# Twenty-eight more fill matmuls in front of batch 0, and another gate for batch 2's q loads

## The chip, the cores and the metric

The kernel runs on one core of a Trainium2 chip. The metric is the device time of one execution in microseconds, as the median of several runs. The engines are named as the profile names them: PE is TensorE (PEld its weight loads), DVE is VectorE, ACT is ScalarE, POOL is GpSimd, and SP is SyncE, which here only issues transfers.

## The reference

Linear attention over 8 batches, 8 heads, 576 positions and 64 columns a head, followed by a normalised two-layer block with a residual:

```
q_s = softmax(q, over head_dim);  k_s = softmax(k, over seq)
kv  = einsum('bhsd,bhse->bhde', k_s, v)
x   = einsum('bhsd,bhde->bhse', q_s, kv)      -> [8, 576, 512]
xn  = (x - mean) / sqrt(var + 1e-6) * g_ln
out = x + relu(xn @ w_ch1) @ w_ch2            w_ch1 [512, 2048], w_ch2 [2048, 512]
```

All inputs and the output are float32 in HBM; the kernel multiplies in bf16.

## The kernel before

**Tiling.** Each batch's first 512 positions form one unit of work ("c", 0 to 7), with position p*4+t on partition p; the remaining 64 positions of all batches form a ninth unit, which runs last. Of a unit, TensorE forms `pkv` (exp of k times v, line 252), VectorE scales it into `kv_sb` (line 260), TensorE forms `po` (exp of q transposed, times `kv_sb`, line 283), VectorE and ScalarE make the normalised `xn`, its transpose is `xnT`, and then come the products with w1 (`ph`, lines 406 and 421, each followed by a relu into `hT`) and with w2 (`pc`, line 466, for unit 0; seven-product form, line 513, for the others).

**Order.** All engines run in the order in which the program is written (a manual schedule). `first_batch()` writes the start by hand. After it, `run()` walks through the steps of one unit's two layers on TensorE, and lets side work of the next units in at given positions: a pair `(96, f)` calls f when the steps so far weigh 96. During unit 0's layers the side work contains unit 1's attention: casts of v at 94 (`cast_v`, line 153, into `vm`; `prep_kvrem`, lines 158 and 159, into `ekr` and `vr`), all of `pkv` at 96 (`kv_all`), `po` from 96.5. At 119 and 127 ScalarE takes the exp of unit 2's q (line 176), and between them, at 126, stands the transpose of unit 1's `xn` whose copy to `xnT` ScalarE makes (line 793).

**The start.** `first_batch()` issues q and k of batch 0 on SP and v, w1 and the rest of q on GpSimd, with small copies into `gate` that make GpSimd wait for q and for k before it issues more. TensorE gets fills: `warm(n)` writes n matmuls of 256 columns of a zero tile `junk` into a bank that nothing reads. There are four groups before unit 0's layers: 32 at the very start; 4 behind each of the two groups of transposes of exp(q) (`eq_pT`, line 791); 10 between `po` and the transposes of `xn` (line 901). Between the second and the third come `gps` (g_ln broadcast to all partitions, line 882), `z` (sums of exp(k), line 229), `pkv`, `po`. Unit 0's layers start with w1's first block of columns for position groups t=0 and t=1, then blocks two to four for t=0,1, and then all blocks for t=2,3.

**The loads after it.** GpSimd's queue takes, in this order: w1's blocks, w2's first two blocks (of four, four row groups each), batch 1's q, k, v and remainders (`load_second`), w2's third and fourth block (`load_w2(2)`, `load_w2(3)`), and then `load_third()`: a one-element copy on GpSimd into batch 2's q tile, and batch 2's v. Batch 2's q and k and their remainders (ktr, vtr) are issued on SP; the q load overwrites what the copy wrote, so it waits for the copy, and what stands behind it on SP waits with it. Batch 2's k and v share their buffers with batch 1's.

Of the kernel before, what the change touches and what calls it, by code (L numbers as in the profile page):

```python
# [20 lines left out]
def kernel(  # L21
# [16 lines left out]
    nc = tc.nc  # L38
# [41 lines left out]
    w2_sb = const.tile([P, KO2, DM], BF16)  # L80
# [9 lines left out]
    def load_w1(nb):  # L90
        cols = slice(nb * 512, nb * 512 + 512)
        nc.gpsimd.dma_start(w1_sb[:, :, cols], w1_src[:, :, cols])

    def load_w2(g4):
        rows = slice(4 * g4, 4 * g4 + 4)
        nc.gpsimd.dma_start(w2_sb[:, rows, :], w2_src[:, rows, :])
# [4 lines left out]
    raws = {}  # L101
# [62 lines left out]
    def new_eq(c):  # L164
        eqs[c] = (
            att.tile([P, T, H, D], BF16, tag="eq", name="eq"),
            sml.tile([P, T, H], FP32, tag="zq", name="zq"),
            sml.tile([P, T, H], FP32, tag="rq", name="rq"),
        )
        eqTs[c] = att.tile([P, T, NP, P], BF16, tag="eqT", name="eqT")  # L170
# [10 lines left out]
    def exp_qt(b, t):  # L181
        if t == 0 and b:
            new_eq(b)
        nc.scalar.activation(eqs[b][0][:, t], raws[b][2][:, :, t], AF.Exp)
# [27 lines left out]
    def exp_k0(j):  # L212
        hs = slice(2 * j, 2 * j + 2)
        if j == 0:
            eks[0] = raw.tile([P, T0, H, D], BF16, tag="vt", name="ek0", bufs=1)
        nc.scalar.activation(
            eks[0][0:P0, :, hs, :].rearrange("p t h d -> p h t d"), raws[0][0][0:P0, hs], AF.Exp
        )

    def k0_mm(j, t):  # L220
        hs = slice(2 * j, 2 * j + 2)
        return eks[0][0:P0, t, hs, :], raws["v0"][0:P0, hs, t, :], P
# [11 lines left out]
    def recip_z(src):  # L234
        rzk = sml.tile([P, 2], FP32, tag="rzk", name="rzk")
        nc.vector.reciprocal(rzk, src)
        return rzk

    def kv_mm(b, j, t):
        par = b % 2  # L240
        last = T if b else T0 - 1
        if j % 2 == 0 and t == 0:
            kvbox["p"] = att_ps.tile([P, 2, 256], FP32, tag="a", name="pkv")
        pkv = kvbox["p"]
        w = P + 1
        if b == 0:
            lhsT, rhs, w = k0_mm(j, t)
        elif t < T:
            lhsT, rhs = eks[b][:, t, 2 * j : 2 * j + 2, :], vm[:, par, t, j, 0 : P + 1]
        else:  # L250
            lhsT, rhs = ekr[:, par, 2 * j : 2 * j + 2, :], vr[:, par, j, 0 : P + 1]
        nc.tensor.matmul(  # L252
            pkv[:, j % 2, 0:w], lhsT, rhs, start=(t == 0), stop=(t == last)
        )
        if j % 2 == 1 and t == last:
            js = slice(j - 1, j + 1)
            rzk = recip_z(pkv[:, :, P]) if b else kvbox["rz", j // 2]
            for half in range(2):
                ps = slice(64 * half, 64 * half + 64)
                nc.vector.tensor_mul(  # L260
                    kv_sb[ps, b, js, ps], pkv[ps, :, ps],
                    rzk[ps].to_broadcast([64, 2, D]),
                )

    def start_x(c):
        xs[c] = (
            mlp.tile([P, T, DM], BF16, tag="x", name="x"),
            mlp.tile([P, T, 6], FP32, tag="st", name="st"),
            mlp.tile([P, T, DM], BF16, tag="xn", name="xn"),
            mlp.tile([P, T, 2], FP32, tag="mv", name="mv"),  # L270
        )
        xnTs[c] = mlp.tile([P, T, KO1, P], BF16, tag="xnT", name="xnT")
# [74 lines left out]
    def mean_x(c, t):  # L347
        nc.scalar.activation(
            scrap, pobox[c, t], AF.Copy, scale=-1.0 / DM, accum_out=xs[c][3][:, t, 0:1]
        )  # L350
# [330 lines left out]
    def warm(n, width=256):  # L681

        w = mm_ps.tile([P, 512], FP32, tag="m", name="warm")
        for _ in range(n):
            nc.tensor.matmul(w[:, 0:width], junk[:, 0:P], junk[:, 0:width], start=True, stop=True)  # L685
# [97 lines left out]
    def norm_q(b, t):  # L783
        eq, zq, rq = eqs[b]
        sum_q(b, t)
        nc.vector.tensor_mul(eq[:, t], eq[:, t], rq[:, t].to_broadcast([P, H, D]))  # L786
# [19 lines left out]
    def eq_pT(c, t, eng):  # L806
        pe_T(eqTs[c], eqs[c][0][:, t].rearrange("p h d -> p (h d)"), t, eng)
# [4 lines left out]
    def first_batch():  # L812

        nc.scalar.preload_act_table_set("natural_log_exp_and_others")
        raws[0] = (
            mlp.tile([P, H, T0, D], FP32, tag="hT", name="kt0", bufs=1), None,
            raw.tile([P, H, T, D], FP32, tag="qt", name="qt"),
        )
        k0, _, q0 = raws[0]
        v0 = mlp.tile([P, H, T0, D], BF16, tag="hs", name="v0", bufs=1)  # L820
        raws["v0"] = v0
        g_row = outp.tile([1, DM], FP32, tag="ot", name="g_row")

        def load_q0(half, eng=nc.sync):
            ts = slice(2 * half, 2 * half + 2)
            eng.dma_start(
                q0[:, :, ts],
                q[0, :, 0:SM, :].rearrange("h (p t) d -> p h t d", t=T)[:, :, ts],
            )

        def src0(x, h0, hn):
            return x[0, h0 : h0 + hn].rearrange("h (p t) d -> p h (t d)", t=T0)

        load_q0(0)
        for h0 in range(0, H, 2):
            nc.sync.dma_start(
                k0[0:P0, h0 : h0 + 2].rearrange("p h t d -> p h (t d)"), src0(k, h0, 2)
            )
            if h0 == 0:
                nc.sync.dma_start(  # L840
                    g_row, bass.AP(moe_g_ln.tensor, moe_g_ln.offset, [[0, 1], [1, DM]])
                )
        nc.vector.memset(junk, 0.0)
        nc.vector.memset(eps_ln, 1e-6)
        nc.vector.memset(ones, 1.0)
        nc.vector.memset(ones_f, 1.0)
        nc.vector.memset(bones, 0.0)
        nc.vector.memset(bones[0:64, 0:1], 1.0)
        nc.vector.memset(bones[64:P, 1:2], 1.0)
        nc.vector.memset(kv_sb, 0.0)  # L850
        make_identity(nc, ident)
        nc.gpsimd.tensor_copy(out=gate, in_=q0[:, 1, 0, 0:4])
        for h0 in (0, 4):
            nc.gpsimd.dma_start(
                v0[0:P0, h0 : h0 + 4].rearrange("p h t d -> p h (t d)"), src0(v, h0, 4)
            )
        nc.gpsimd.tensor_copy(out=gate[0:P0], in_=k0[0:P0, 5, 0, 0:4])
        load_w1(0)
        load_q0(1, nc.gpsimd)
        for nb in range(1, 4):  # L860
            load_w1(nb)
        load_w2(0)
        load_w2(1)

        new_eq(0)
        start_x(0)
        warm(32)
        for t in range(2):
            exp_qt(0, t)
            norm_q(0, t)  # L870
        exp_k0(0)
        nc.vector.memset(vr[:, :, :, P:], 1.0)
        nc.vector.memset(vr[:, :, :, 0:P], 0.0)
        nc.vector.memset(ekr, 0.0)
        nc.vector.memset(vm[:, :, :, :, P:], 1.0)
        exp_k0(1)
        for t in range(2):
            eq_pT(0, t, nc.scalar)
            exp_k0(2 + t)
            warm(4)  # L880
        gps = mm_ps.tile([P, DM], FP32, tag="m", name="gps")
        nc.tensor.matmul(gps, ones_f, g_row, start=True, stop=True)
        nc.vector.tensor_copy(out=g_bc, in_=gps)
        for j in range(NP):
            z0_mm(j)
        for h in range(2):
            kvbox["rz", h] = recip_z(kvbox["z0", h][:, :, 0])
        for j in range(NP):
            for t in range(T0):
                kv_mm(0, j, t)  # L890
        for t in range(2):
            for i in range(NP):
                po_mm(0, t, i)
        xn, mv = xs[0][2], xs[0][3]
        stats(0, 0, pobox[0, 0], (slice(0, DH2), slice(DH2, DM)))
        mean_x(0, 1)
        warm(10)
        for i in range(2):
            ptr = mm_ps.tile([P, 2, 2 * P], BF16, tag="m", name="ptr")
            for j in range(2):  # L900
                nc.tensor.transpose(ptr[:, j, 0:P], xn[:, 0, (2 * i + j) * P : (2 * i + j + 1) * P], ident)
            nc.scalar.copy(xnTs[0][:, 0, 2 * i : 2 * i + 2], ptr[:, :, 0:P])  # L902
        xn_sub(0, 1)
# [13 lines left out]
    def load_third():  # L917

        alloc_batch(2)
        nc.gpsimd.tensor_copy(out=raws[2][2][0:1, 0, 0, 0:1], in_=raws[1][1][0:1, 0, 0, 0:1])  # L920
        load_main(nc.gpsimd, 2, 1, 0, H)
        for which in (2, 0):
            load_main(nc.sync, 2, which, 0, H)
        load_kvrem(nc.sync, 2)
# [118 lines left out]
```

## Time and profile before

| | |
|---|---|
| runs, us | 282.18, 282.10, 282.39, 283.70, 282.99 |
| median, us | 282.39 |
| profiled execution, us | 282.18 |
| its span, us | 280.4 |
| mean granted TensorE clock | 0.988 |
| busy: PE, PEld, DVE, ACT, POOL, us | 271.6, 199.5, 196.5, 181.9, 32.3 |
| HBM read, written | 36.70 MB, 9.44 MB |

The span runs from the first to the last instruction that the profile shows; the execution's own time is 1.78 us longer. All times below are microseconds from the span's start. Software queue q0 holds what GpSimd issues, hardware queue q1 what SP issues. The granted clock is a share of TensorE's full speed.

### The profile page before, as it was taken

How to read it: one execution, taken by the hardware profiler on the slowest of the kernel's cores; microseconds unless marked ns; L12 is line 12 of the kernel's file. 1: busy time of each engine (PE TensorE's matmuls, PEld its weight loads, DVE VectorE, ACT ScalarE, POOL GpSimd, SP SyncE). 2: the span in 40 equal slices, each digit the busy share in tenths (PEclk: the TensorE clock that was granted, in tenths of full speed). 3: DMA queues.
4: the chain of work that ended last, by engine and by line, in shares of the span. 5: the costliest groups of instructions: out<-in, count | busy, mean ns of one | idle time of the engine just before them, and what ended most of it. 6: DMA issues, size and time to landing. Idle time of an engine off the chain costs nothing.

```text
span 280.4 us, 5551 instructions
## 1 busy us (share of the span) xinstructions
PE 271.6 (97%) x2197; PEld 199.5 (71%) x2200; DVE 196.5 (70%) x452; ACT 181.9 (65%) x344; POOL 32.3 (12%) x58
## 2 busy tenths in 40 slices
PE   7889999999999999999999999999999999999993
PEld 5678855656995599658965896589659855885683
DVE  4646578957996688658865886588657929952363
ACT  4446872798885986688659865986585477536500
POOL 3752001300020003000300030003000300030000
PEclk9779999999999999999999999999999999999999
DMA  7999999999779965994599449954916510141014
GB/s 188 217 234 209 356 230 324 293 225 358 111 177 273 296 110 148 301 256 84 143 300 252 96 139 294 264 96 119 219 38 68 143 54 4 37 140 49 0 40 112
DMA packets 69580, 49.06 MB, mean 175 GB/s; under 512 B 41201, under 2 KB 66289, under 8 KB 69554
## 3 DMA queue, kind: packets, MB, share of 16 engines
q1 hardware_dynamic: 60050, 30.02, 47.0%
q0 software_dynamic: 8912, 18.16, 25.1%
q10 hardware_dynamic: 592, 0.52, 0.6%
q8 instruction: 17, 0.28, 0.4%
q14 instruction: 9, 0.07, 0.1%
HBM read 36.70 MB, written 9.44 MB: 165 GB/s over the span
## 4 chain that ended last, share of the span: by engine, by line
PE 94%; DVE 2%; DMA 2%; ACT 0%; issue 0%
PE ph L406 30%; PE ba L513 20%; PE ph L421 15%; PE bb L513 5%; PE bc L513 5%; PE be L513 5%; PE pc L466 5%; PE pkv L252 4%; PE po L283 3%; DMA qt<-in_q_dram 2%; PE ptr L791 1%; PE warm L685 1%; DVE kv_sb L260 1%; PE po L290 1%; DVE eq L786 0%; DVE zq L192 0%
## 5 line engine op out<-in xcount | busy, mean ns | idle before, releaser
L406 PE MATMUL ph<-xnT,w_sb 128*128 128x512 bf16 x384 | 90.6, 379 | 0.0
L394 ACT ACTIVATE hT<-ph 128x512 bf16<-128x512 f32 x96 | 54.8, 598 | 16.3 <-PE ph L406 16.3
L406 PEld LDWEIGHTS <-w_sb 128*128 128x128 bf16 x384 | 35.6, 98 | 36.6
L513 PEld LDWEIGHTS <-hs 128*128 128x128 bf16 x512 | 49.1, 98 | 5.8 <-DVE hs L497 0.2
L421 PE MATMUL ph<-xnT,w_sb 128*128 128x256 bf16 (+1 forms) x400 | 49.1, 268 | 0.3 <-ACT xnT L902 0.3
L431 ACT ACTIVATE hT<-ph 128x512 bf16<-128x512 f32 x44 | 25.7, 596 | 25.1 <-PE ph L421 25.1
L497 DVE TENSOR_TENSOR hs<-hT 128x1024 bf16<-128x1024 bf16 x32 | 21.9, 688 | 28.6 <-ACT hT L394 28.5
L513 PEld LDWEIGHTS <-hT 128*128 128x128 bf16 x384 | 36.6, 98 | 5.3 <-ACT hT L394 0.2
L421 PEld LDWEIGHTS <-w_sb 128*128 128x128 bf16 x400 | 35.3, 98 | 4.0 <-issue 0.4
L530 POOL DMA_DIRECT2D out_dram<-ot x28 | 15.1, 542 | 181.9 <-DVE ot L524 181.9
L513 PE MATMUL ba<-w_q,hs 128*128 128x256 bf16 x256 | 31.3, 273 | 0.0
L323 DVE SCALAR_TENSOR_TENSOR xn<-x,mv,g_bc 128x512 bf16<-128x512 bf16 x34 | 25.6, 752 | 1.2
L283 PE MATMUL po<-kv_sb,eqT 128*128 128x128 bf16 x128 | 24.6, 224 | 1.0 <-DVE kv_sb L260 1.0
L330 DVE SCALAR_TENSOR_TENSOR x<-po,rq 128x512 bf16<-128x512 f32 x30 | 20.6, 686 | 7.0 <-PE po L283 6.8
L317 ACT ACTIVATE scrap<-x,mv 128x512 bf16<-128x512 bf16 x34 | 24.6, 722 | 0.4 <-DVE mv L336 0.2
L252 PE MATMUL pkv<-vm,ek 128*128 128x129 bf16 x112 | 21.7, 220 | 0.0
L538 ACT COPY s<-ba 128x512 f32<-128x512 f32 x15 | 8.8, 586 | 15.9 <-PE ba L513 15.6
L283 PEld LDWEIGHTS <-eqT 128*128 128x128 bf16 x128 | 11.8, 101 | 8.3 <-issue 1.5
L176 ACT ACTIVATE eq<-qt 128x1024 bf16<-128x1024 f32 x14 | 14.6, 1056 | 4.0 <-DMA qt<-in_q_dram 2.4
L732 DVE TENSOR_REDUCE zq<-eq 128x8 f32<-128x512 bf16 x26 | 16.3, 693 | 0.0
L513 PE MATMUL ba<-w_sb,hT 128*128 128x256 bf16 x128 | 16.3, 273 | 0.0
L513 PE MATMUL bc<-w_sb,hT 128*128 128x256 bf16 x128 | 15.7, 273 | 0.0
(122 smaller groups left out, 338.4 us busy)
## 6 DMA issues: line engine op xcount, KB each, us to landing
out_dram<-ot POOLq DMA_DIRECT2D x32, 256.0 KB, 2.9
qt<-in_q_dram SPq DMA_DIRECT2D x6, 1024.0 KB, 7.7
kt<-in_k_dram SPq DMA_DIRECT2D x6, 1024.0 KB, 10.5
vt<-in_v_dram SPq DMA_DIRECT2D x5, 1024.0 KB, 13.0
w_sb<-in_moe_w_ch_dram POOLq DMA_DIRECT2D x8, 512.0 KB, 13.4
vt<-in_v_dram POOLq DMA_DIRECT2D x2, 1024.0 KB, 16.2
kt<-in_k_dram SPq DMA_DIRECT2D x4, 288.0 KB, 5.5
qt<-in_q_dram POOLq DMA_DIRECT2D x1, 1024.0 KB, 18.5
```

The source lines that it names most:

```text
L252: nc.tensor.matmul(pkv[:, j % 2, 0:w], lhsT, rhs, start=(t == 0), stop=(t == last))
L283: nc.tensor.matmul(pobox["p"][:, i * P : i * P + P], eqTs[c][:, t, i, :], kv_sb[:, c, i, :], start=True, stop=True,)
L317: nc.scalar.activation(scrap, x[:, t], AF.Square, bias=mv[:, t, 0:1], accum_out=mv[:, t, 1:2])
L323: nc.vector.scalar_tensor_tensor(xn[:, t], in0=x[:, t], scalar=mv[:, t, 0:1], in1=g_bc, op0=ALU.add, op1=ALU.mult)
L330: nc.vector.scalar_tensor_tensor(x[:, t].rearrange("p (h d) -> p h d", h=H), in0=pobox[c, t].rearrange("p (h d) -> p h d", h=H), scalar=1. ...
L394: nc.scalar.activation(dst, src, AF.Relu)
L406: nc.tensor.matmul(hbox["ph"], w1_sb[:, ko, m * P : (m + 1) * P], xnTs[c][:, :, ko, :], start=(ko == 0), stop=(ko == KO1 - 1),)
L421: nc.tensor.matmul(ph[:, m % 2, at : at + tn], w1_sb[:, ko, m * P : (m + 1) * P], xnTs[c][:, t0 : t0 + tn, ko, :], start=(ko == 0), stop=( ...
L431: nc.scalar.activation(dst, ph, AF.Relu)
L497: nc.vector.tensor_tensor(out=dst, in0=x, in1=y, op=op)
L513: nc.tensor.matmul(hbox[bank][:, t], lhsT, rhs, start=first and (own or t == 0) and k == 0, stop=k == KH - 1, skip_group_check=True)
L732: s = spread([lambda t=t: nc.vector.reduce_sum(zq[:, t], eq[:, t], axis=AX.X) for t in range(T)][t0:], 0, 12)
```

## The change

Five places. The first group of fills has 44 matmuls instead of 32. The two groups behind the transposes of exp(q) have 12 and 5 instead of 4 and 4. A new group of 6 stands between `pkv` and `po` of batch 0. The group between `po` and the transposes of `xn` has 11 instead of 10. These are 28 more matmuls of 256 columns in all: 12, 8, 1, 6 and 1 in the order of the program. The one-element copy on GpSimd that holds back batch 2's loads reads an element of w2's third block (row group 8) instead of an element of batch 1's v.

```
-        warm(32)
+        warm(44)
         for t in range(2):
             exp_qt(0, t)
             norm_q(0, t)
...
         for t in range(2):
             eq_pT(0, t, nc.scalar)
             exp_k0(2 + t)
-            warm(4)
+            warm((12, 5)[t])
...
         for j in range(NP):
             for t in range(T0):
                 kv_mm(0, j, t)
+        warm(6)
         for t in range(2):
             for i in range(NP):
                 po_mm(0, t, i)
         xn, mv = xs[0][2], xs[0][3]
         stats(0, 0, pobox[0, 0], (slice(0, DH2), slice(DH2, DM)))
         mean_x(0, 1)
-        warm(10)
+        warm(11)
...
     def load_third():

         alloc_batch(2)
-        nc.gpsimd.tensor_copy(out=raws[2][2][0:1, 0, 0, 0:1], in_=raws[1][1][0:1, 0, 0, 0:1])
+        nc.gpsimd.tensor_copy(out=raws[2][2][0:1, 0, 0, 0:1], in_=w2_sb[0:1, 8, 0:1])
         load_main(nc.gpsimd, 2, 1, 0, H)
         for which in (2, 0):
             load_main(nc.sync, 2, which, 0, H)
         load_kvrem(nc.sync, 2)
```

More of the change, by code (lines that the diff above doesn't have):

```diff
@@ L866, in first_batch @@
         start_x(0)
-        warm(32)
+        warm(44)
         for t in range(2):
@@ L879, in first_batch @@
             exp_k0(2 + t)
-            warm(4)
+            warm((12, 5)[t])
         gps = mm_ps.tile([P, DM], FP32, tag="m", name="gps")
@@ L890, in first_batch @@
                 kv_mm(0, j, t)
+        warm(6)
         for t in range(2):
@@ L896, in first_batch @@
         mean_x(0, 1)
-        warm(10)
+        warm(11)
         for i in range(2):
@@ L919, in load_third @@
         alloc_batch(2)
-        nc.gpsimd.tensor_copy(out=raws[2][2][0:1, 0, 0, 0:1], in_=raws[1][1][0:1, 0, 0, 0:1])
+        nc.gpsimd.tensor_copy(out=raws[2][2][0:1, 0, 0, 0:1], in_=w2_sb[0:1, 8, 0:1])
         load_main(nc.gpsimd, 2, 1, 0, H)
```

## The prediction

> **What bounds the kernel now.** I read the chain that ended last, then the engines by stretches of the first 18 us, then the order of time around 40 to 45 us, then the DMA issues with their landings. Chain in order of time (start, length, what):
>
> ```profile
> 9.37 0.44 PE warm L685 x4
> 9.81 1.05 PE gps L882 x2
> 10.86 0.71 PE z L229 x24
> 11.57 2.60 PE pkv L252 x24
> ...
> 14.83 0.80 PE po L283 x6
> 15.63 2.13 PE warm L685 x10
> ```
>
> TensorE carries the start from 9.0 us on. Batch 0's 24 pkv products take 108 ns each; the same line at 42.37 us takes 58 ns (0.58 us for 10). The engines by stretches say why (length, busy time and count of each engine, then clock and DMA); the first two rows hold the fills alone (what reads junk), the last two everything:
>
> ```profile
> 4.33:7.75 3.42, 2.08 (x19) 1.68 (x18) 0.00 (x0) 1.00 1.09 272
> 7.75:11.16 3.41, 1.10 (x8) 0.55 (x6) 0.00 (x0) 1.00 1.27 212
> ```
> ```profile
> 11.16:14.57 3.41, 3.20 (x42) 3.04 (x39) 1.56 (x7) 0.00 (x0) 3.41 (x6) 0.50 1.22 235
> 14.57:17.99 3.42, 3.16 (x20) 2.53 (x20) 2.63 (x6) 0.69 (x2) 2.49 (x3) 0.50 1.17 237
> ```
>
> The clock is 0.50 from 11.16 to 17.99 us and 1.00 elsewhere (stretches of 0.1 us give 0.80 for 11.1 to 11.2 and 0.57 for 17.9 to 18.0). I cut the time before the fall into stretches of half that length: one with 2.08 us of fills was followed by full clock, one with 1.10 us by half clock.
>
> What the start is worth depends on what it meets. Order of time, 40 to 45 us (start, length, [idle before <- who ended it]):
>
> ```profile
> 40.44 1.43 DVE L153 CAST vm<-vt 128x512 bf16<-128x512 f32 x4 [1.37 <-DMA vt<-in_v_dram]
> ...
> 41.90 0.42 DVE L159 CAST vr<-vtr 64x512 bf16<-64x512 f32 x1
> ...
> 42.43 0.22 PE L252 MATMUL pkv<-vr,ekr 128*128 128x129 bf16 x1
> ...
> 44.65 0.49 PE L283 MATMUL po<-kv_sb,eqT 128*128 128x128 bf16 x6 [0.54 <-DVE kv_sb L260]
> ```
>
> Batch 1's v is late already: VectorE idles 1.37 us for it, casts until 42.32, and the first product that needs vr starts at 42.43. The chain shows no wait of TensorE there, but only about 0.06 us hide it: a semaphore from VectorE to TensorE costs 0.04 to 0.05 (kv_sb ends 44.61, po starts 44.65), so 42.37 was possible. From 44.65 the chain is TensorE almost without a gap until 276 us, so what is lost or won at 42.4 reaches the end in full. Its cause (DMA issues; the last figure is us from issue to landing):
>
> ```profile
> vt<-in_v_dram POOLq DMA_DIRECT2D x1, 1024.0 KB, 23.3
> ```
>
> Issued at 17.14, landed at 40.44, behind the weights and batch 1's q and k in the same queue.
>
> **The change, part by part.** The sum is against the profiled execution: span 280.4 and 1.78 around it, 282.18 us, 0.21 under the median 282.39. A fill streams 0.109 us at full clock (0.44 for 4) and 0.213 at half (2.13 for 10).
>
> *44 first fills for 32.* The 32 end at 6.31 as recorded and about 6.14 as streamed; 12 more stream to 7.45. The transposes behind them waited for VectorE until 7.42: +0.03 us, hidden, since ScalarE is busy until 8.21.
>
> *12 and 5 for 4 and 4.* The first group streams from 7.68 to 8.99; the next transposes waited for VectorE until 8.97, so +0.02. The fifth fill ahead of gps is uncovered: +0.11. gps, z and pkv start 0.13 later: pkv at about 11.7, less 0.06 since z stays at its early pace: 11.64.
>
> *The clock.* The stretch 7.75 to 11.16 then holds about 2.0 us of fills (1.24 and 0.55 streamed, each group with 0.16 of latency), nearer to the 2.08 row than to the 1.10 row, so I take the clock to stay. Then pkv takes 24 x 0.058 = 1.39 and ends at 13.03 against 14.17. Batch 0's second v block landed at 5.98 + 6.3 = 12.28, and its first use comes at 12.34: no wait, by 0.06. kv_sb (0.6 after pkv) lets po go on at about 13.8 against 14.83.
>
> A rule speaks against this. The Trainium skill (TensorE: Matmul & The Clock Gate, "Why this matters for your kernels") has the clock fall after an idle window, from gaps over some 3 us. By that rule the row above would not have fallen at all, its longest gap being 1.11 us, and the fills would buy nothing; the row decides.
>
> *6 fills between pkv and po.* 0.65 us, 13.03 to 13.68, inside the wait for kv_sb until 13.8: nothing at full clock, 0.9 at half (see rivals).
>
> *11 fills for 10.* po's stage has 0.13 less work at full clock, so statistics start at 14.1 against 15.24. The xn halves (VectorE, 0.88 us from 16.19) end 1.39 and 1.83 after that start: 15.5 and 15.9. The fills run from 14.15 to 15.35 and no longer hold up the transposes (before, to 17.77, 0.7 past the second half of xn). Batch 0's products run in earnest from about 17.0 against 18.93: 1.9 us earlier.
>
> *What is late next: w1.* Issued at 10.69, 11.43 and 12.16 with 8.8, 10.7 and 12.5 us to landing, w1's second to fourth blocks land at 19.49, 22.13 and 24.66. Their first products started at 20.95, 23.34 (4 fills' length into the run of 20 at 22.90) and 25.31: cover 1.46, 1.21 and 0.65. No load before 40 us is moved by the change, so of 1.9 us at most 0.65 - 0.04 = 0.61 passes the fourth block.
>
> *Then v.* TensorE comes to batch 1's pkv at about 41.6, does four products and waits for vr until 42.37. ekr (ScalarE, 41.72 to 42.35) moves forward with its transposes and doesn't bind. The gain kept is 0.06 us.
>
> *The gate.* GpSimd's one-element copy opens the q load of batch 2. It read vt (40.44) and now reads w2's third block, which landed at 24.95 + 18.6 = 43.55: 3.1 us later, not earlier. Behind it on GpSimd stands batch 2's v load (issued 42.43; now about 44.0, +1.5; wanted at 59.03, landed 51.5). Behind it on SP stand q (40.94, now 44.05), k, ktr, vtr, then the transposes of eq (issued 55.10). What it could win is w2's third block sooner, and the loads by queue say no (packets, MB, time in 16 engines' share), first for 40.5 to 42, then for 43.4 to 47:
>
> ```profile
> q0 software_dynamic: 308, 0.30, 122.7%
> ```
> ```profile
> q1 hardware_dynamic: 1036, 1.05, 83.2%
> q0 software_dynamic: 173, 0.19, 28.7%
> ```
>
> q1, where q's load stands, moved nothing in the first stretch, though issued at 40.94. And a sooner block only meets the wait for kv_sb (43.77 to 44.65). The Trainium skill (DMA: Bandwidth & Descriptors, "Queues, rings and completion order") has the engines go round the queues packet by packet; by that w2's block would have lost half the rate to q, and the gate would bring it about 1 us forward (an estimate); the sum would not move, as kv_sb binds.
>
> What it can cost: q's first bytes came at about 43.4 and will come at 44.05 + 1.2 (the first load of the kernel: issued 0.74, bytes from about 1.9) = 45.2. Meanwhile w2's last 0.19 MB need 0.55 us, so the engines lose at most 1.25 us. The bytes are the same; q lands between 52.14 (40.94 + 11.2), or sooner, and 53.4. ScalarE's exp of q started at 52.59; the xnT copy behind it ended 54.12 and is needed when TensorE has done 16 products from 53.26, at 55.0: cover 0.85 with the semaphore. Cost 0 to 0.4; below nothing is excluded, since TensorE doesn't wait there. I take 0, the middle of the delay (0.6) being under the cover. k landed at 56.43; the products that use it start at 60.7, after exps ending at 59.0: cover 1.7.
>
> Sum: 282.18 - 0.06 + 0 = 282.1.
>
> **Rivals.**
>
> *Slower: q of batch 2 comes late by the gate's whole 3.1 us.* exp of q at 55.7, xnT at 57.2, TensorE waits 2.2: 284.3. It decides from a landing later than about 53.0. For it: q, k and the remainders all queue behind the gate, and ScalarE waited 1.09 for that q already. Against: the bytes of q1 were held up until 43.4 anyhow.
>
> *The fills don't hold the clock.* It still falls at 11.16: +0.13 ahead of z; pkv ends at 14.30; six fills take 1.28; po's last six start about 0.9 later; the eleventh fill adds 0.2. Then 1.1 us late, and nothing later gives it back: 283.2. For it: the groups still end at 9.8, and gps and z follow as before.
>
> *Faster: v doesn't bind.* If v lands some 0.6 earlier, w1's cap holds: 281.6. If w1's blocks come earlier too, the whole 1.9: 280.3. Against: all these loads are issued by GpSimd on gates that the change leaves alone.
>
> **How the numbers follow.** Forecast 0.62 (its own range 281.8 to 282.5); v not binding 0.10; neither v nor w1 0.06; clock not held 0.10; q late 0.12. Leaving out the two ends (0.18), the range is 281.4 to 283.6. Half a percent, 1.4 us, is about what a measurement of this kernel can tell from no change. Faster by more: 0.06. Slower by more: q late and a little of its neighbours, 0.13. Between: 0.81.
>
> **What would show it.** Right: clock 1.00 from 11.2 to 18.0; pkv of batch 0 at about 58 ns; TensorE idle before w1's blocks at 19.5, 22.1 and 24.7 and before pkv at 42.4; vt landing within 0.1 of 40.44; po at 44.6; q of batch 2 issued near 44.0. Wrong: po of batch 1 well before 44.5; or an idle TensorE near 55 us that DMA qt ended at ScalarE; or a clock of 0.50 after 11.2 us.

## The result and the profile after

The changed kernel took 284.52 us (median of 33 runs, 282.13 to 287.38), the kernel before, beside it on the same chips, 282.93 (59 runs, 281.59 to 284.82). The ratio is 1.0057, 95% interval 1.0041 to 1.0073: slower by about 1.6 us. The forecast was no change at 282.1, and its range ended at 283.6. The profiled execution of the changed kernel took 283.12 (span 281.3), 1.4 under its own median; two more profiles further down show slower executions of it. All ratios are taken over the runs within 1.5% of the fastest of their kernel, so that one can differ a little from the quotient of the two medians.

**The start.** Engines by stretches (length, busy time and count of PE, PEld, DVE, then clock, DMA, GB/s): first the fills alone, what reads `junk`, then everything.

```profile
4.33:7.75 3.42, 3.42 (x23) 2.62 (x22) 0.00 (x0) 1.00 1.09 273
7.75:11.16 3.41, 3.13 (x26) 2.18 (x24) 0.00 (x0) 1.00 1.29 213
```
```profile
11.16:14.57 3.41, 3.41 (x56) 2.59 (x56) 1.85 (x7) 0.66 (x1) 3.41 (x5) 1.00 1.17 209
```

The clock stays at 1.00 where it was 0.50 before. But the second row holds 3.13 us of fills where about 2.0 were forecast, because the first group ran late. Order of time on TensorE:

```profile
1.06 7.64 PE L685 MATMUL warm<-junk 128*128 128x256 bf16 x44 [1.06 <-DVE junk L843]
8.54 0.39 PE L791 MATMUL ptr<-ident,eq 128*128 128x128 bf16 x4
```

There is no bracket behind the transposes: nothing but the fills held them. VectorE had finished exp(q) at 7.74 (7.05 + 0.69, line 786), so TensorE was 0.8 us late at its first useful work.

**The gate.** The chain that ended last, in order of time:

```profile
25.12 18.19 DMA w_sb<-in_moe_w_ch_dram
...
43.44 0.19 POOL qt L921
...
44.13 13.98 DMA kt<-in_k_dram
...
58.14 1.06 ACT ek L143
```

Before, this stretch of the chain was TensorE's, apart from VectorE's work on `kv_sb` from 42.98 to 44.61. Now it is w2's third block, the gate's copy, and batch 2's k. What TensorE and its neighbours made of it (order of time):

```profile
44.34 0.49 PE L283 MATMUL po<-kv_sb,eqT 128*128 128x128 bf16 x6 [0.50 <-DVE kv_sb L260]
54.86 1.91 PE L421 MATMUL ph<-xnT,w_sb 128*128 128x256 bf16 x16 [0.17 <-ACT xnT L793]
58.14 1.06 ACT L143 ACTIVATE ek<-kt 128x1024 bf16<-128x1024 f32 x1 [0.91 <-DMA kt<-in_k_dram]
60.17 0.42 DVE L159 CAST vr<-vtr 64x512 bf16<-64x512 f32 x1 [1.52 <-DMA vtr<-in_v_dram]
61.14 0.22 PE L252 MATMUL pkv<-vm,ek 128*128 128x129 bf16 x1 [0.27 <-ACT hT L394]
```

TensorE came to `po` 0.31 us earlier than before (44.34 against 44.65) and then idled 0.17 for `xnT`, whose copy stood behind the exp of a late q, and 0.27 behind the exp of a late k.

### The profile page after: what moved, and what is told of

The parts are those of the page before. It is cut to its first block, busy times and chain, and to the rows that moved or that the text cites. A ratio compares the mean times of both kernels' runs of the same rounds, so it can differ in the third digit from the quotient of the medians.

```text
span 281.3 us, 5605 instructions
## 1 busy us (share of the span) xinstructions
PE 273.7 (97%) x2225; PEld 200.7 (71%) x2228; DVE 196.7 (70%) x452; ACT 182.2 (65%) x344; POOL 32.2 (11%) x58
## 4 chain that ended last, share of the span: by engine, by line
PE 66%; DMA 21%; DVE 5%; ACT 4%; POOL 1%; issue 1%; SPq 1%; DVEq 0%; ACTq 0%; POOLq 0%
PE ph L406 24%; PE ba L513 17%; DMA w_sb<-in_moe_w_ch_dram 11%; PE ph L421 7%; DMA kt<-in_k_dram 7%; PE bb L513 4%; PE bc L513 4%; PE be L513 4%; DMA qt<-in_q_dram 3%; PE pkv L252 2%; ACT hT L394 2%; DVE hs L497 2%; PE po L283 1%; DVE ot L524 1%; POOL w_sb L92 1%
## 5 line engine op out<-in xcount | busy, mean ns | idle before, releaser
L283 PE MATMUL po<-kv_sb,eqT 128*128 128x128 bf16 x128 | 24.0, 219 | 0.5 <-DVE kv_sb L260 0.5
L466 PE MATMUL pc<-w_sb,hT 128*128 128x512 bf16 x61 | 15.4, 379 | 0.3 <-DMA w_sb<-in_moe_w_ch_dram 0.2
```

Of the source, the lines that this page charges most:

```text
L283: nc.tensor.matmul(pobox["p"][:, i * P : i * P + P], eqTs[c][:, t, i, :], kv_sb[:, c, i, :], start=True, stop=True,)
```

## The experiments

All ratios are against the kernel before, on the same chip, with 95% intervals.

**The two parts apart.** All new fills with the old gate; the new gate with the old fills.

```
e1_fills:  changed kernel, but in_=raws[1][1][0:1, 0, 0, 0:1]   (the old gate)
e2_gate:   kernel before, but  in_=w2_sb[0:1, 8, 0:1]           (the new gate)
```

> All new fills, the old gate (an element of batch 1's v). Theory A (the loss comes from the loads behind the gate): q of batch 2 issued near 41, landing near 52, ScalarE's wait for it about 1 us as before; time against before 0 to -0.4 us (ratio 0.9985 to 1.000), because v of batch 1 still binds at 40.4. Theory B (the loss comes from the first group of 44, which runs on past VectorE's work when the clock rises late): TensorE's first transposes about 1 us late, pkv of batch 0 later too, time +1 to +1.6 us (ratio 1.004 to 1.006).

> Fills as before, only the new gate (an element of w2's third block). Theory A: q of batch 2 issued near 43.7 to 44, k landing near 58 instead of 56.4, ScalarE waiting for both, TensorE waiting for xnT near 55 and for relus near 61; time +1 to +2 us (ratio 1.004 to 1.007), the whole of the changed kernel's loss. Theory B: within 0.3 us of before (ratio 0.999 to 1.001).

e1: 284.39, 1.0058 [1.0034, 1.0083]. e2: 284.06, 1.0051 [1.0024, 1.0078]. Each part alone costs as much as both together, so the prices don't add. The profile of e2, with the old fills, is at full clock from 11 to 18 us too: the fall that the prediction wanted to take away is not in every execution. Half the clock from 11.16 to 17.99, 6.83 of 280.4 us, makes a mean clock of 0.988. Among the 117 runs of the kernel before that e1, e5, e9 and e13 were compared with, 67 had a mean clock under 0.992 (median 282.93) and 24 had 0.995 or more (median 282.40): the fall costs about 0.5 us, and with this scatter anything between 0.1 and 0.9 is possible.

e2's own profile (283.20) shows none of its 1.4 us behind the gate: TensorE waited there for no load of batch 2. What the gate does is read from the runs of the next sections and from the profiles of the changed kernel.

**Which fills.** e1 with 32 first fills; the kernel before with 44 or 60 first fills and nothing else; later e1 with 60, and the kernel before with 44, 12 and 5.

```
e3_fills_first32:  e1 with warm(32)
e5_first44:        kernel before with warm(44)
e6_first60:        kernel before with warm(60)
e9_fills_first60:  e1 with warm(60)
e10_44_and_12_5:   kernel before with warm(44) and warm((12, 5)[t])
```

> The fills of the changed kernel except that the first group stays at 32, the old gate. Theory A: like the kernel with all fills, 0 to -0.4 us against before. Theory B: 1 to 1.6 us faster than the kernel with all fills, so 0 to -0.4 us against before while that one is slower.

> The kernel before with the first group of fills at 44 instead of 32 and nothing else. If the 12 fills cost by themselves (they run on past the moment when VectorE has exp(q) ready): +1 to +1.6 us (ratio 1.0035 to 1.0057). If they cost only together with the other new groups, whose in-order fills leave TensorE no slack to catch up: 0 to +0.4 us (ratio 1.000 to 1.0015). If the difference between the two earlier kernels was scatter: within 0.3 us of before.

> The kernel before with the first group of fills at 60, a larger dose of the same. If the 12 cost by themselves through TensorE's order, 16 more at 0.11 us add their full 1.7 us: +2.8 to +3.4 us in all (ratio 1.010 to 1.012), with the first transposes near 10 us instead of 7.4 to 7.8. If the waits for w1 and v cover delays of the start: under +1.2 us (ratio under 1.004).

> All new fills with 60 instead of 44 in the first group, the old gate. Theory (the first group runs past the exps of q, and with 12, 5, 6 and 11 behind it the start of TensorE has no idle time that takes the lateness up): 16 more fills are 1.74 us more, of which the later waits for w1 and vr (0.31 to 1.4 us together in the runs so far) take up a part: ratio 1.007 to 1.011 against the kernel before, and the profile shows first transposes of exp(q) at 9.6 us or later. Rival (the cost of the 44 alone in company of the other fills is scatter of the landings; w1 and vr take the lateness up): at most 1.004, as with 60 alone (1.0038).

> The kernel before with 44 first fills and 12 and 5 behind the transposes; no six, ten and not eleven, the old gate. Theory (12 and 5 take away the 0.72 us of idle time ahead of the second transposes, and so the lateness of 44 passes on): 1.003 to 1.006, like all fills with 44 (1.0058). Rival (it takes the six and the eleventh fill too, or it was scatter): 1.000 to 1.002, like 44 alone (1.0005) and like the other fills with 32 (1.0006).

e3: 1.0006 [0.9986, 1.0026]. e5: 1.0005 [0.9982, 1.0028]. e6: 1.0038 [1.0018, 1.0059]. e9: 1.0035 [1.0011, 1.0060]. e10: 1.0028 [1.0003, 1.0053]. So with the old gate the fills behind the first group win and lose nothing that shows (e3), and 44 alone don't either (e5), but 44 with others behind them, or 60, cost 0.3 to 0.6%. That 12 and 5 behind the 44 make the difference isn't shown: the intervals of e5 and e10 overlap, and e10 lies between its two expectations. The theory of the dose fell: 60 with the other fills (1.0035) were not slower than 44 with them (1.0058), and the two intervals overlap. What the first fills cost beside the old gate is about 1 us; where exactly it is lost stays open (below).

**The gate's dose.** The old fills and a gate one block later, on w2's fourth.

```
e4_gate_later:  kernel before, but in_=w2_sb[0:1, 12, 0:1]
```

> Fills as before; the gate reads w2's fourth block, which lands some 3.3 us after the third (46.85 against 43.55 in the trace of before). Theory A: q issued near 47, q and k landing 2 to 3 us later than with the third block, little of it covered: +3.5 to +5 us against before (ratio 1.012 to 1.018). Theory B: no loss (ratio 0.999 to 1.001).

288.50, 1.0156 [1.0106, 1.0205]. q was issued at 47.41 and TensorE idled 4.26 us, for k, not for q (order of time):

```profile
62.82 1.06 ACT L143 ACTIVATE ek<-kt 128x1024 bf16<-128x1024 f32 x1 [5.46 <-DMA kt<-in_k_dram]
...
65.82 0.22 PE L252 MATMUL pkv<-vm,ek 128*128 128x129 bf16 x1 [4.26 <-ACT hT L394]
```

**What makes q and k late: a gap, and v in the other queue.** The queues in the changed kernel (packets, MB, time in 16 engines' share), for 44.65 to 48.65 and for 50.65 to 51.65:

```profile
q1 hardware_dynamic: 1020, 1.03, 84.0%
q0 software_dynamic: 42, 0.05, 6.2%
```
```profile
q0 software_dynamic: 77, 0.32, 82.7%
q1 hardware_dynamic: 77, 0.08, 23.3%
```

Batch 2's q (1.05 MB, in q1) had just not been moved in full when v's bytes, issued by GpSimd 0.35 us after q, began to move in q0, at about 48.6. In the second of these stretches both queues move as many packets, but v's are of 4 KB (0.32 MB in 77) and q's and k's of 1 KB, so q1 falls from 0.35 MB a microsecond to 0.08 until v is through. There are two kinds of executions under the new gate. In e12 (below) q1 moved 1.17 MB in the four microseconds ahead of v, not 1.03: q was through, and landed 5.5 us after its issue, k 11.5. In the changed kernel q's last bytes stood beside v's: 9.2 us, and k 14.0.

This is not new, though. In the kernel before, q1 moved 1.03 MB from 42.9 to 46.9, and then v stood beside q and k in the same way, here from 47 to 48:

```profile
q0 software_dynamic: 73, 0.30, 84.0%
q1 hardware_dynamic: 80, 0.08, 25.9%
```

There q landed 11.2 us after its issue and k 15.0, no sooner than in the changed kernel, and both were still in time. What the new gate adds is a gap ahead of q: until it opens no load of batch 2 is issued, and until their bytes come the engines have only the end of w2 to move. All packets from 43 to 48, in the kernel before, the changed kernel and its third profile (e16, below):

```profile
DMA packets 1445, 1.71 MB, mean 342 GB/s; under 512 B 29, under 2 KB 1361, under 8 KB 1445
DMA packets 1081, 1.09 MB, mean 218 GB/s; under 512 B 16, under 2 KB 1081, under 8 KB 1081
DMA packets 653, 0.65 MB, mean 129 GB/s; under 512 B 23, under 2 KB 653, under 8 KB 653
```

At 0.35 MB a microsecond, the rate of q1 alone, the difference is an estimated 1.8 and 3.0 us of lost transfer (e15, also below: 0.71 MB, 2.9 us; e2: 0.80 MB, 2.6 us; e4: 0.38 MB, 3.8 us; e1, e3, e14 and e17, with the old gate, moved 1.48 to 1.64 MB). So q and k are late by the gap and by v together; a kernel with only one of the two (the kernel before has v, e11 below the gap) loses nothing.

So the next kernels take v out of the way: batch 2's v is issued on SP behind k.

```
-        load_main(nc.gpsimd, 2, 1, 0, H)
-        for which in (2, 0):
+        for which in (2, 0, 1):
             load_main(nc.sync, 2, which, 0, H)

e7_v_behind_k:                   the changed kernel with this edit
e8_first32_old_gate_v_behind_k:  e3 with this edit (32 first fills, old gate)
e11_gate_v_behind_k:             e2 with this edit (old fills, new gate)
e13_first32_v_behind_k:          e7 with warm(32)
e14_old_gate_v_behind_k:         the kernel before with this edit
```

> The changed kernel with batch 2's v load moved from GpSimd's queue to SP's, behind k. If k's landing at 58 is made late by v and the stores in the other queue (theory: the gate costs because q and k then share the engines with v): q lands 6 to 7 us after its issue and k 8 to 9, so near 50 and 53; ScalarE waits for neither; the gate's part of the loss, 1 to 1.3 us, goes (ratio to before 1.000 to 1.004). If k is late from its issue alone: no better than the changed kernel (ratio 1.0055).

> First group at 32, the other new fills, the old gate, and batch 2's v load on SP behind k. A candidate to beat both kernels: ScalarE's wait for q of batch 2 (1.1 us in the trace of before) goes, TensorE did not wait for it there, so 0 to -0.6 us against before (ratio 0.998 to 1.000), with less scatter upward. If v then comes too late (wanted at 59): VectorE waits for vt near 59 and the time is above before.

> The kernel before with the new gate, and batch 2's v load on SyncE's queue behind k instead of on GpSimd's. Theory (the gate costs through k, which shares the engines with v): k lands at 55 to 56 instead of 58 us, no idle time of ScalarE for kt, ratio 1.000 to 1.002 against 1.0051 for the gate alone. Rival (the gate costs through q, or by the 3 us by which all of batch 2 moves): 1.004 to 1.006.

> The changed kernel with 32 first fills and with batch 2's v on SyncE's queue behind k; the other new fills and the new gate stay. Theory (the 44 cost 0.3 to 0.5% where the other fills stand behind them, the gate costs only through k beside v): 0.997 to 1.001 against the kernel before, at least 0.25% below the same kernel with 44 (1.0034). Rival (the 44 cost nothing, the other fills or the gate do): 1.002 to 1.005, as with 44.

> The kernel before with batch 2's v on SyncE's queue behind k, and nothing else. Theory (with the old gate k lands in time beside v as well, so there is nothing to win): 0.998 to 1.001, like the same with the new gate (0.9985). Rival (v behind k is a gain of its own that hid the gate's price of 0.5% there): 0.992 to 0.996.

e11: 282.51, 0.9985 [0.9965, 1.0005], against 1.0051 with the same gate and v on GpSimd. e14: 0.9990 [0.9966, 1.0014], so the edit is no gain of its own; with the old gate k lands in time either way. Without v beside them q and k make up for the gap, which e11 has as well (1.05 MB from 43 to 48). So under the old fills the gate costs only as long as v stands beside k; v's share costs nothing by itself, since under the old gate the cover (how late a load may land before anyone waits for it) takes it up. In e11 q lands after 6.6 us and k after 9.1, and from 49.01 to 53.01 q1 holds its rate:

```profile
q1 hardware_dynamic: 1383, 1.40, 107.0%
```

With the new fills the edit gave back a part at most: e7 1.0034 [1.0006, 1.0062], e13 1.0040 [1.0012, 1.0068], e8 (old gate) 1.0003 [0.9982, 1.0025]. The 12 first fills make no difference there (e13 against e7), against my expectation. A second profile of e13, e18 below, shows one way in which it still loses; the first shows no wait for a load of batch 2.

**The changed kernel with 32 first fills.**

```
e12_after_first32:  the changed kernel with warm(32)
```

> The changed kernel with 32 instead of 44 in the first group; the new gate stays. Theory (two causes, the 44 in company of 12 and 5, and the gate, which cover each other as waits one behind the other): the gate is left, 1.004 to 1.006. Rival (the loss of the whole change is that of the fills, and the gate costs only where the start is late too): 1.000 to 1.002.

284.42, 1.0055 [1.0027, 1.0084]: beside the new gate, the 12 first fills cost nothing on top.

**More profiles.** The profiles of the changed kernel, e1 and e13 were faster than the medians of their kernels, so these three were profiled again, unchanged, the changed kernel twice.

```
e15_after_again, e16_after_third:  the changed kernel
e17_fills_again:                   e1
e18_e13_again:                     e13
```

> The changed kernel once more, for a second profile. Theory (k of batch 2 is late): a run near the median, 284.5, idles 1 to 2 us on TensorE between 60 and 67 us behind ScalarE's wait for kt. Rival (late loads of v, vtr and w2's third block): po of batch 1 starts at 45.5 or later and from there on takes the 236.9 us of the first profile.

> The changed kernel a third time; the same as for the second. Both profiles together should show one of the two waits in the slower of them.

> All new fills with the old gate, for a second profile. Theory (the loss of the fills lies ahead of po of batch 1, in late loads that bind in any case): po at 45.2 or later, and 236 us from there. Rival (it lies behind, at batch 4's q near 98 us): over 0.4 us of idle time of TensorE there.

> 32 first fills, the other new fills, the new gate and v behind k, for a second profile. Theory (the loss lies ahead of po of batch 1): po at 45.2 or later, no wait for q or k. Rival (behind it): idle time near 98 us of 0.5 us or more, with po at 44.5.

They took 285.90, 286.70, 284.23 and 285.69 us; the first two lie in the upper third of the changed kernel's 33 runs, and only two of those are slower than e16. The third profile of the changed kernel, order of time on ScalarE and TensorE:

```profile
56.84 1.06 ACT L176 ACTIVATE eq<-qt 128x1024 bf16<-128x1024 f32 x1 [3.95 <-DMA qt<-in_q_dram]
58.42 1.91 PE L421 MATMUL ph<-xnT,w_sb 128*128 128x256 bf16 x16 [2.02 <-ACT xnT L793]
...
102.17 1.16 PE L513 MATMUL ba<-w_sb,hT 128*128 128x256 bf16 x9 [0.79 <-ACT hT L394]
```

Here q was issued at 45.70 and took 10.7 us. In the second profile (e15) q and the remainder of v were late:

```profile
56.44 1.91 PE L421 MATMUL ph<-xnT,w_sb 128*128 128x256 bf16 x16 [0.49 <-ACT xnT L793]
...
62.38 0.42 DVE L159 CAST vr<-vtr 64x512 bf16<-64x512 f32 x1 [2.15 <-DMA vtr<-in_v_dram]
63.20 0.22 PE L252 MATMUL pkv<-vm,ek 128*128 128x129 bf16 x1 [0.75 <-DVE vm L153]
```

And in e18, with v behind k, the remainders behind v in the same queue are late instead: ScalarE idles 1.11 us for ktr, VectorE 2.88 for vtr, TensorE 0.86 at 63.13.

These profiles lose time in three places; what the sum leaves of the excess, 0.1 to 0.5 us, is not placed. The table has the start of the third group of `po` of batch 1 (products 9 to 12) against 45.72 before; TensorE's waits for batch 2's loads (47 to 66 us); its wait at about 100 us; their sum; and the time less the 282.18 of the profile before.

| profile | time | po | batch 2 | at 100 | sum | excess |
|---|---|---|---|---|---|---|
| changed kernel | 283.12 | -0.32 | 0.44 | 0.29 | 0.41 | 0.94 |
| e15, the same | 285.90 | 0.95 | 1.24 | 0.99 | 3.18 | 3.72 |
| e16, the same | 286.70 | 1.39 | 2.02 | 0.79 | 4.20 | 4.52 |
| e1, fills | 283.30 | 0.52 | 0 | 0.42 | 0.94 | 1.12 |
| e17, the same | 284.23 | 0.64 | 0 | 1.29 | 1.93 | 2.05 |
| e2, gate | 283.20 | 0.96 | 0 | 0 | 0.96 | 1.02 |
| e11, gate, v behind k | 282.73 | 0.28 | 0 | 0.18 | 0.46 | 0.55 |
| e18, e13 again | 285.69 | 1.41 | 0.86 | 0.95 | 3.22 | 3.51 |
| e14, v behind k alone | 284.56 | 1.63 | 0 | 0.65 | 2.28 | 2.38 |

*po.* It scatters by 2 us with and without each part (e14 has neither the fills nor the new gate), with the landings of v, vtr and w2's third block, all in one queue. *Batch 2.* This column is the gate's: none of the profiles with the old gate (before, e1, e3, e5, e6, e8, e9, e10, e14, e17) has an entry, and five of the ten with the new gate or the later one have one (the changed kernel's three, e4, e18). *At 100.* This is batch 4's q, which ScalarE needs ahead of its relus. Over all profiles its landing up to 7.8 us after its issue (before: 7.3) makes TensorE wait nothing, after 8.0 us 0.29, 8.2 us 0.46, 8.5 us 0.79, 8.7 us 0.99, 9.0 us 1.29: a cover that ends between 7.7 and 7.8 us, past which each microsecond counts in full. It comes in kernels with neither part as well (e14: 8.3 us, 0.65). e17 and e18 lose at *po* and at 100 both, where their expectations had set one against the other.

**The best version.** None beats the kernel before beyond the measurement: e11 (0.9985) and e14 (0.9990) can't be told from it. e11 beats the changed kernel; their intervals lie apart.

## Why the prediction was wrong

Two terms of the sum failed, and the runs with one of the two parts alone (e1 the fills, e2 the gate) are slower by about as much as the whole change: the gate, put at 0, and the 44 first fills, put at 0.03 us. For the first the runs show what happened; for the second they show only that it costs.

**The fills behind the first group: right.** The clock stayed at 1.00, batch 0's 24 `pkv` took 1.50 us as recorded (1.39 as streamed was forecast), the six fills lay inside the wait for `kv_sb`. The start that this bought was worth little, as the sum had it (0.06 us); executions of the kernel before that don't have the fall are about 0.5 us faster. That the amount of fills in the stretch (2.08 us or 1.10) decides was argued from two rows; e2 kept the clock with the old fills, and in e18, with the new ones, it fell to 0.87 and 0.63. Neither my threshold nor the rule that I set against it (the Trainium skill, TensorE: Matmul & The Clock Gate, "Why this matters for your kernels": a fall after idle gaps of over some 3 us) tells these executions apart, since none of their gaps is that long.

**"44 first fills: +0.03 us, hidden": wrong in size.** It took the pace of the 32 fills of one profile. The pace changes from 0.213 to 0.109 us a fill when the clock rises; from the groups' lengths that was at about 4.3 us in the profile before, but at 6.5 in the changed kernel (44 fills in 7.64 us) and 6.8 in e12 (32 in 6.47). In e5 and e15 it was at 4.0, and there the 44 ended at 7.45 as forecast. In the first profile the 44 ended 0.8 us past VectorE, and batch 0's products began in earnest at 17.9 instead of the forecast 17.0 (18.8 before). By the runs 44 cost nothing alone (e5) or beside the new gate (e12), and 44 or 60 with 12 and 5 behind them and the old gate cost 0.3 to 0.6% (e1, e9, e10). That it is the late end of the group that costs isn't shown: e15 ended it in time and took 285.90.

**w1 and v as the next waits: right.** TensorE waited 0.31 us for w1's fourth block in the changed kernel and 0.73 and 0.37 for the second and fourth in e15. vr's first product came at 42.12 (42.37 forecast) because v landed at 40.19 and not 40.44; in e15 and e16 TensorE waited 0.90 and 0.38 for vr. So of the early start almost nothing passes, as the sum had it: e3 is at 1.0006. "And a sooner block only meets the wait for kv_sb" was incomplete: in e15, e16 and e17 TensorE waited 0.37 to 0.58 us for w2's third block itself.

**"The gate: cost 0 to 0.4, I take 0": wrong, and this is the step whose failure the runs explain.** The gate costs 1.4 us by e2, and as much by e12 against e3 (1.0055 and 1.0006), which differ in it alone. Three assumptions failed. First, the gate's time: 43.55, 3.1 us past v, was one execution's figure; w2's third block landed at 43.32, 44.83 and 45.39 in the three profiles, and q was issued at 43.65, 45.12 and 45.70. Second, "the engines lose at most 1.25 us", so that q lands by 53.4: they lost 1.8, 2.9 and 3.0 us, and q landed at 52.85, 54.4 and 56.4. Behind that gap v, wanted last, stood beside q and k and took 70 to 80% of the bytes, as it had before. The prediction's own row shows that it missed this: 1.05 MB, the size of q, had gone through q1 by 47, yet q landed at 52.14. Third, k's cover of 1.7 us, which the sum set against no delay of k: k's landing moved from 56.43 to 58.11 in the first profile and to 59.6 and 61.3 in the others, and ScalarE waited for it in all three.

The rule on queues that I weighed there (the Trainium skill, DMA: Bandwidth & Descriptors, "Queues, rings and completion order": an engine takes turns between queues, packet by packet) agrees with the row of 77 packets against 77. I had set it aside because of a stretch in which q1 moved nothing, up to 1.1 us behind q's issue. That need not be two ready queues: in e4 q's first bytes came 0.8 us after its issue with nothing else to move, and the full rate only after 2 us. Why they took 2.4 us in the kernel before stays open.

**The slower rival: right in kind.** "q late by the whole 3.1 us" named the place, the limit (a landing past 53.0) and the wait (2.2 us); the third profile has the landing at 56.4 and the wait of 2.02. In the others the delay came partly through q (0.17 and 0.49 us) and partly through k and vtr (0.27 and 0.75). Its chance of 0.12 was too low: each of the four loads behind the gate on SP moved later, and one had 0.85 us of cover.

**Open.** Why 44 first fills cost about 1 us beside the old gate and nothing beside the new one; why v behind k heals the gate under the old fills (0.9985) but not fully under the new (1.0034, 1.0040). One lead was not followed. The prediction has "No load before 40 us is moved by the change", but GpSimd issued batch 1's v at 17.1 to 17.7 us in the five profiles with the old fills, and at 18.1 to 19.3 in twelve of the fifteen with more; v landed 0.4 us later there on average. It can't be the whole answer, since e3 has it (18.78) and loses nothing. The profiles place the losses at late loads of batch 1 and at batch 4's q, which also scatter without the edits. That waits for transfers follow one another, so that a TensorE that is late already waits less at the next, would explain why the prices don't add; it is argued, not shown.

## What to carry to other kernels

A later gate delays everything behind it in every queue that it opens. Before it is costed at nothing, write down for how long the engines will have little to move until the first bytes behind it come, and set that against the cover of every load behind it, not of the first alone. Here a load with small packets beside one with large packets got the small share of the bytes; putting both into one queue, in the order in which they are wanted, paid for the gap under the old fills and was worth nothing with the old gate. And covers of under a microsecond are not to be trusted from one profile when transfers scatter by one to two.

## What the runs showed of the hardware

- The same load of v moves in 4 KB packets when GpSimd issues it (247 packets, 0.98 MB in 48.65 to 52.65 us of the changed kernel) and in packets of about 1 KB when SP does (e11, 49.01 to 53.01: 1383 packets, 1.40 MB, q1 alone, with the ends of q and k). Beside each other the queues moved about equal packets, not equal bytes (77 and 77, 73 and 80).
- The rise of TensorE's clock at the start comes at about 4.0 us (e5, e15) to 7.0 us (e3, e7) in different executions, an estimate from the length of the first group of fills and the two paces. The column of granted clock doesn't show it.
- The fall of the clock at about 11 us comes and goes between executions of the same start (0.50 in the kernel before, 1.00 in e2), and costs this kernel about 0.5 us.
